# A float32 delta-rule recurrence with an MLP behind it: 128-wide TensorE products and transposes recast as 64x64 tiles, with PSUM handed out in four pairs of banks

## The chip, the cores and the metric

The kernel runs on one core of one Trainium2 chip. The metric is device time in microseconds of one execution, median of several runs. TensorE is called PE below, its weight loads PEld, VectorE DVE, ScalarE ACT, GpSimd POOL and SyncE SP.

## The reference, cut to what matters

```python
batch, n_heads, seq, head_dim = (4, 8, 768, 40)
for t in range(S):
    y[:, :, t] = np.einsum('bhd,bhde->bhe', rt, state)
    Sa = np.einsum('bhde,bhe->bhd', state, at)
    state_decay = state * wt[:, :, None, :] - np.einsum('bhd,bhe->bhde', Sa, bt)
    state = state_decay + np.einsum('bhd,bhe->bhde', vt, kt)
...
x = attn_out.transpose(0, 2, 1, 3).reshape(3072, 320)
h = x @ w_in                                  # 320 x 1024
e = np.exp(h - np.max(h, -1, keepdims=True))
solu = h * e / (np.sum(e, -1, keepdims=True) + 1e-09)
ln = (solu - mean) / np.sqrt(var + 1e-06) * g_ln
out = ln @ w_out                              # 1024 x 320
```

r, k, v, w, a and b are float32, the MLP's weights float64; the output is 3072 x 320 in float32.

## The kernel before, in words

The sequence is cut into chunks of 64 steps. One piece of work i is one chunk of a pair of batches: two batches times 64 steps fill the 128 partitions, and there are 24 pieces (12 chunks times two pairs, in turn). Within a chunk the recurrence is written as products of matrices. A unit of such a product is one batch p and one head (q, g, h); its operands take 64 partitions or 40, and its result 64 partitions, so 16 units go to the array as 64x64 tiles, four at a time. in_turn() (line 256) orders the units so that four neighbours lie in four different quadrants. mm() (line 264) issues such a product. Each float32 product shows as two matmul records and two weight loads in the trace; a transpose (nc.tensor.transpose) as one of each.

The steps of a piece, by their functions and the tiles that they write:

- logged(), decay() (322, 326): lw = log of the decay, pcum = its running sum over the chunk (one 128x128 product of 320 columns), ei = exp of it and inv = exp of its negative.
- turned() (347): four 128x128 transposes that bring a token-major tile to feature-major. It serves decay_turned() (pei, to ex), front() (pa, to aT on DVE), front_b() (pb, to bT), attend_kv() and attend_r() (pk, pv, pr, to kT, vT, rT on ACT). stated() (505) turns the state in the same way (pst, to s).
- norm() (394): pnt, masked into nt on DVE, which goes to DRAM; spread() and invert() bring it back as blocks and invert a triangular matrix on DVE in 30 steps of two instructions each (lines 436 and 438, tiles prod and uu) for two pieces at once. some() doles these steps out to given places in DVE's order: 3 or 0, then 5, 4, and 5 or 4 in each iteration.
- flip(), couple(), close() (461, 467, 480): tu turned on DVE, py to wy on ACT, pz to tu.
- scores() (518): ps, masked into psi and lv on DVE. carried() and driven() (536, 552): px, which becomes x0 on ACT. solved() (564): pu, to nuT and lu on ACT. answered() (583): pl, masked on DVE into the other half of lu. read() (594): pyo, in two halves (own and not own) with fence(), a drain of PE, between them; it reads s, lv and lu. leave() (618): x and the new state's total tot on DVE, the state on POOL; x goes by DMA to xT.
- The MLP, 128 tokens at a time: hidden() (661) makes h from two 128-row blocks and one 64-row block of w_in, six products of 512 columns; highest(), exped(), weighed(), spreadof() (673 to 709) are the row maximum nmax (DVE), e = exp (ACT), e = h*e (DVE) and the statistics bs, mv, c (DVE) and rs (POOL); folded() (711) turns e by eight 128x128 transposes into lnT; output() (723) makes po by eight 128x128 products of 320 columns, in two halves, and osb (ACT), which is stored.
- narrow(), split() (208, 177): the float64 weights are narrowed to float32 by bit operations on DVE and ACT, in the prologue and in iterations -1 to 3.

The order of every engine is written by hand: each engine executes in the order in which the functions are called (manual_schedule). The main loop (line 823) runs i from -1 to 27. Iteration i works at once on pieces i (solved, answered, read, leave), i+1 (scores, couple, close, carried, driven), i+2 (by_value, attend), i+5 to i+7 (front, norm, decay) and the MLP of earlier ones. In it, PE goes through pu, ps, pst, pa, h, pb, pei, h, pcum, po, py, pnt, pl, po, pz, pyo (own), px, h (64 rows, two products), drain, pyo (not own), px, plnT, h, pk, pv, h, pr. DVE goes through psi, lv, aT, steps, tu, nmax, steps, nt, lu, e, bs, mv, c, steps, x, tot, steps.

PSUM has eight banks. ps1 gives pairs of banks in two buffers to all 64x64 products (banks()), ps2 one pair to h, pcum of early pieces and the mean, ps3 single banks in two buffers to transposes, pcum and po (bank()). A product that takes a buffer waits until the buffer's former content has been read.

Of the kernel before, what the change touches and what calls it, by code (L numbers as in the profile page):

```python
# [17 lines left out]
P = 128  # L18
# [9 lines left out]
THIN = (5, 15)  # L28
# [23 lines left out]
def kernel(  # L52
# [34 lines left out]
    ps1 = ctx.enter_context(tc.tile_pool(name="ps1", bufs=2, space=PSUM))  # L87
    ps2 = ctx.enter_context(tc.tile_pool(name="ps2", bufs=1, space=PSUM))
    ps3 = ctx.enter_context(tc.tile_pool(name="ps3", bufs=2, space=PSUM))
# [30 lines left out]
    ei_t = zeroed(nc.vector, "ei", [P, H, C], 1, pad)  # L120
# [18 lines left out]
    def banks(name):  # L139
        return ps1.tile([P, 2, 512], FP32, tag="banks", name=name)  # L140

    def bank(name):
        return ps3.tile([P, 512], FP32, tag="bank", name=name)
# [76 lines left out]
    def turn_g():  # L220
        pg = bank("pg")
        nc.tensor.transpose(out=pg[:, 0:NF], in_=g_rows, identity=ident[0:NF, 0:NF])
        for x, y in zip(g_cols, (0, -20, -36)):
            nc.scalar.mul(out=x, in_=pg[:, 0:NF], mul=2.0 ** y)
# [6 lines left out]
    def mean_of(lo, hi, begun):  # L231
        t = bank("pmean")
# [33 lines left out]

    def fence():
        nc.tensor.drain()  # L270
# [51 lines left out]
    def logged(i):  # L322
        lw = st[i]["lw"] = two.tile([P, DM], FP32, tag="lw", name="lw", bufs=1)
        nc.scalar.activation(out=lw, in_=st[i]["raw_w"].rearrange("p h d -> p (h d)"), func=AF.Ln)

    def decay(i):
# [5 lines left out]
        t = (bank("pcum") if i > 5 else ps2.tile([P, DFF], FP32, tag="h", name="h"))[:, 0:DM]  # L332
        nc.tensor.matmul(t, lhsT=c_("cum"), rhs=d["lw"], start=True, stop=True)  # L333
        nc.scalar.activation(out=ei_t[0][:, :, 0:D], in_=heads(t), func=AF.Exp)
# [12 lines left out]
    def turned(name, x):  # L347
        t = bank("p" + name)
        for j in range(4):
            nc.tensor.transpose(out=t[0:W2, j * P:(j + 1) * P],  # L350
                                in_=x[:, 2 * j:2 * j + 2].rearrange("p a b -> p (a b)")[:, 0:W2], identity=ident)
        return t[0:W2].rearrange("p (j b t) -> p b j t", j=4, b=2)

# [3 lines left out]
    def kept(name, t, bufs=1):  # L357
        o = tokens(name, bufs)
        nc.scalar.copy(out=o[0:W2], in_=t)
        return o  # L360

    def decay_turned(i):
        if not ok(i):
            return
        ex = st[i]["ex"] = ex_t[i % (AHEAD + 2)]
        nc.scalar.copy(out=ex[0:W2, :, :, 1:], in_=turned("ei", ei_t[0]))

    def front(i):
        if not ok(i):
            return  # L370
        d = st[i]
        t = turned("a", d["raw_a"])
        aT = d["aT"] = tokens("aT", AHEAD)
        nc.vector.tensor_tensor(out=aT[0:W2], in0=t, in1=d["ex"][0:W2, :, :, 0:C], op=ALU.mult)

    def front_b(i):
        if not ok(i):
            return
        d = st[i]
        d["bT"] = kept("bT", turned("b", d["kb"][:, H:]))  # L380
# [13 lines left out]
    def norm(i):  # L394
# [3 lines left out]
        t = banks("pnt")  # L398
# [68 lines left out]
    def couple(i):  # L467
# [3 lines left out]
        t = banks("py")  # L471
# [8 lines left out]
    def close(i):  # L480
# [3 lines left out]
        t = banks("pz")  # L484
# [8 lines left out]
    def attend_kv(i):  # L493
        if not ok(i):
            return
        d = st[i]
        d["kT"] = kept("kT", turned("k", d["kb"]))
        d["vT"] = kept("vT", turned("v", v_t[0]))

    def attend_r(i):  # L500
        if not ok(i):
            return
        st[i]["rT"] = kept("rT", turned("r", r_t[0]), 2)

    def stated(i):
        if not ok(i):
            return
        d = st[i]
        bp, ci = where_(i)
        if ci:  # L510
            t = bank("pst")
            for x in range(4):
                nc.tensor.transpose(out=t[0:W2, x * P:(x + 1) * P],  # L513
# [418 lines left out]
```

## Time and profile before

| what | value |
|---|---|
| median of 3 runs | 620.01 us (620.0, 620.01, 626.2) |
| span of the profiled execution, first to last instruction | 616.2 us (the page lists no other time for it) |
| mean granted clock of PE in it | 0.928 |
| start of pu in iterations 0, 5, 18, 23 | 65.8, 183.0, 464.5, 561.6 us |
| transfers | 59.93 MB, mean 97 GB/s |
| the queue that brings PE's instructions (q8) | 90 packets, 1.47 MB |

The profiled execution is a separate one from the timed ones: durations and places in time are read from it, and the median is compared with the timed runs of the changed kernel. The page gives busy time and number of instructions of each engine, the span in 40 slices with the clock that PE was granted, DMA queues, the chain of work that ended last, and groups of instructions with their mean time and the idle time before them. Ends of matmuls are modelled and overlap; their starts are measured. In a line of the timeline, the columns are start, duration, engine, line, operation, output and inputs, shapes and how many were merged; a bracket gives idle time before it and who ended it. In the table by stage the columns are the stretch, its length, and for PE, PEld, DVE, ACT and POOL the busy time and number of instructions, then the granted clock, the DMA engines' share and GB/s.

### The profile page before, as it was taken

The page shows a single profiled execution, that of the slowest core. Times are in us where ns is not written, and L with a number is a line of the kernel's source. Part 1 is how long each engine was busy: PE and PEld are TensorE (multiplying, and loading weights), DVE is VectorE, ACT ScalarE, POOL GpSimd, SP SyncE. Part 2 cuts the span into 40 slices and gives each one's busy share as a digit, 9 for nine tenths or more (in the row PEclk, how much of TensorE's full clock was granted, in tenths as well). Part 3 has the DMA queues.
Part 4 walks back from the last instruction along what each step waited for, and adds up shares of the span by engine and source line. Part 5 has one row for each costly group of instructions (what it writes and reads, how often), then busy time and mean ns, then how long its engine had stood idle before and what let it go on. Part 6 is the DMA issues. An engine that isn't in the chain of part 4 may idle for free.

```text
span 616.2 us, 26656 instructions
## 1 busy us (share of the span) xinstructions
PE 552.0 (90%) x11453; PEld 401.9 (65%) x11453; DVE 449.0 (73%) x1262; ACT 265.8 (43%) x548; POOL 258.0 (42%) x424
## 2 busy tenths in 40 slices
PE   5555668889999999999999999999999999999994
PEld 3333457666676777777777777777777676676652
DVE  4797986988968869869868868788697588443431
ACT  3433444654543544454444445444433343342221
POOL 3463264283453472473365355444624631322200
PEclk9665765789999999999999999999999999999998
DMA  7986887476455455564564474564532622310100
GB/s 164 159 156 121 183 157 129 98 156 104 76 106 104 90 115 99 93 122 95 100 123 91 95 126 98 112 113 82 110 56 53 118 49 43 65 35 26 28 19 21
DMA packets 213901, 59.93 MB, mean 97 GB/s; under 512 B 199120, under 2 KB 208952, under 8 KB 213784
## 3 DMA queue, kind: packets, MB, share of 16 engines
q1 hardware_dynamic: 195512, 33.78, 32.8%
q0 software_dynamic: 11568, 19.78, 14.0%
q10 hardware_dynamic: 6704, 4.67, 2.7%
q8 instruction: 90, 1.47, 1.0%
q14 instruction: 27, 0.22, 0.1%
HBM read 40.10 MB, written 13.37 MB: 87 GB/s over the span
## 4 chain that ended last, share of the span: by engine, by line
PE 74%; DVE 17%; ACT 3%; issue 3%; DMA 1%; ACTq 1%; DVEq 0%; SPq 0%
PE po L731 16%; PE h L265 16%; PE pyo L265 8%; DVE uu L438 5%; DVE prod L436 5%; PE pu L265 4%; PE plnT L720 4%; PE ps L265 4%; PE px L265 3%; PE py L265 2%; PE pl L265 2%; PE pz L265 2%; PE pr L350 2%; PE pst L513 2%; PE pcum L333 1%
## 5 line engine op out<-in xcount | busy, mean ns | idle before, releaser
L265 PE MATMUL h<-w_in,xT 128*128 128x512 f32 (+1 forms) x288 | 123.7, 614 | 0.0
L731 PE MATMUL po<-w,lnT 128*128 128x320 f32 x384 | 112.7, 438 | 0.5 <-ACT lnT L721 0.5
L438 DVE TENSOR_TENSOR uu<-uu,prod 128x30 f32<-128x30 f32 (+4 forms) x360 | 102.1, 284 | 12.4
L436 DVE TENSOR_TENSOR prod<-blk,uu 128x30 f32<-128x30 f32 (+4 forms) x360 | 99.2, 276 | 9.6
L731 PEld LDWEIGHTS po<-w,lnT 128*128 128x128 f32 x384 | 71.0, 190 | 32.6 <-issue 4.1
L409 POOL DMA_DIRECT2D nt_dram<-nt x20 | 18.8, 938 | 120.8 <-DVE nt L383 99.8
L709 POOL TENSOR_TENSOR rs<-c,mhalf 128x1 f32<-128x1 f32 x24 | 13.5, 561 | 112.3 <-DVE c L708 103.4
L383 DVE TENSOR_TENSOR psi<-ps,cst 128x512 f32<-128x512 f32 x24 | 16.6, 690 | 59.5 <-PE ps L265 59.5
L658 POOL DMA_DIRECT2D xT<-x x96 | 48.9, 514 | 0.4 <-DMA blk<-nt_dram 0.3
L265 PEld LDWEIGHTS h<-w_in,xT 128*128 128x128 f32 (+1 forms) x288 | 37.6, 190 | 9.4 <-issue 8.1
L678 DVE TENSOR_REDUCE nmax<-h 128x1 f32<-128x1024 f32 x24 | 28.6, 1193 | 18.6 <-PE h L265 18.6
L420 POOL DMA_DIRECT2D blk<-nt_dram x46 | 36.9, 808 | 11.8 <-issue 8.4
L265 PE MATMUL pyo<-lv,kb 64*64 64x104 f32 x768 | 38.3, 269 | 2.2
L265 PEld LDWEIGHTS pyo<-lv,kb 64*64 64x64 f32 x768 | 24.1, 142 | 21.2 <-issue 21.1
L265 PE MATMUL pyo<-lu,kb 64*64 64x104 f32 x768 | 37.4, 262 | 0.1
L646 POOL TENSOR_TENSOR st<-tot,ex 104x160 f32<-104x160 f32 x44 | 21.7, 511 | 36.4 <-DVE tot L642 32.4
L562 ACT COPY x<-px 128x320 f32<-128x320 f32 x24 | 10.2, 426 | 56.3 <-PE px L265 56.1
L477 ACT ACTIVATE wy<-py,cst 128x256 f32<-128x256 f32 x24 | 11.4, 474 | 53.2 <-PE py L265 53.2
L288 POOL DMA_DIRECT2D raw_r<-in_r_dram x48 | 33.9, 709 | 0.0
L735 ACT ACTIVATE osb<-po,rs 128x320 f32<-128x320 f32 x24 | 12.7, 527 | 48.5 <-PE po L731 32.8
L686 ACT ACTIVATE e<-h,nmax 128x1024 f32<-128x1024 f32 x24 | 26.6, 1108 | 14.3 <-DVE nmax L678 14.3
L692 DVE TENSOR_TENSOR e<-h,e 128x1024 f32<-128x1024 f32 x24 | 29.2, 1217 | 4.7 <-ACT e L686 4.7
(131 smaller groups left out, 1169.1 us busy)
## 6 DMA issues: line engine op xcount, KB each, us to landing
blk<-nt_dram POOLq DMA_DIRECT2D x46, 128.0 KB, 4.7
nt_dram<-nt POOLq DMA_DIRECT2D x20, 256.0 KB, 3.7
raw_w<-in_w_dram SPq DMA_DIRECT2D x48, 80.0 KB
a<-in_a_dram SPq DMA_DIRECT2D x48, 80.0 KB
raw_r<-in_r_dram POOLq DMA_DIRECT2D x48, 80.0 KB, 3.6
lv<-in_v_dram SPq DMA_DIRECT2D x48, 80.0 KB
out_dram<-osb ACTq DMA_DIRECT2D x24, 160.0 KB
raw_b<-in_b_dram SPq DMA_DIRECT2D x44, 80.0 KB
```

Of the source, the lines that this page charges most:

```text
L265: nc.tensor.matmul(o, lhsT=lhsT, rhs=rhs, start=start, stop=stop, skip_group_check=True)
L288: queue.dma_start(out=x[half(p), :, 0:D], in_=ap[2 * bp + p, :, ci * C:(ci + 1) * C, :].rearrange("h t d -> t h d"))
L420: queue.dma_start(out=nb[home:home + Q], in_=blocks[n][:, Q * e:Q * e + Q, Q * e:Q * e + Q])
L436: nc.vector.tensor_tensor(out=t, in0=nb[:, j:j + 1, j + 1:Q].to_broadcast([P, n_c, m]), in1=u[:, 0:n_c, j:j + 1].to_broadcast([P, n_c, m]) ...
L438: nc.vector.tensor_tensor(out=u[:, 0:n_c, j + 1:Q], in0=u[:, 0:n_c, j + 1:Q], in1=t, op=ALU.subtract)
L646: nc.gpsimd.tensor_tensor(out=to3(old), in0=to3(tot[0:W2]), in1=ex[:, :, 2 * q:2 * q + 2, C:].to_broadcast([W2, 2, 2, D]), op=ALU.mult)
L658: nc.gpsimd.dma_start(out=xT[to:to + Q, 2], in_=x[at + P - 3 * D:at + D, 2])
L678: nc.vector.tensor_reduce(out=nmax, in_=d["h"], axis=AX.X, op=ALU.max, negate=True)
L686: nc.scalar.activation(out=e, in_=d["h"], func=AF.Exp, bias=d["nmax"], accum_out=d["esum"])
L692: nc.vector.tensor_tensor(out=d["e"], in0=d["h"], in1=d["e"], op=ALU.mult)
L720: nc.tensor.transpose(out=t[:, j * P:(j + 1) * P], in_=d["e"][:, f * P:(f + 1) * P], identity=ident)
L731: nc.tensor.matmul(d["out"][:, 0:DM], lhsT=d["lnT"][:, f, :], rhs=w2[:, f, :], start=f == 0, stop=f == NF - 1)
```

## The change

All but a few PE instructions become 64x64 products through mm(); left as they were are the mean of w_out and the turn of g_ln.

- turned(), stated() and folded() no longer transpose: each 64x64 (or 64x40) block is multiplied with a 64x64 identity, 16 products in place of four transposes, and 32 in place of eight for e. The source of the decay's turn is lw itself, with the running-sum matrix in place of the identity, so the turn and the sum are one product; ACT then takes exp while copying to ex, and ei is gone. decay() still makes pcum for inv, by two half-sized products into one bank.
- hidden() makes each of five waves of four 64-row, 64-token products of 512 columns, each in its own quadrant, the two row halves into different banks; output() makes 16 waves of four products of 160 columns in two phases, between which row halves and banks are exchanged, with a fence() ahead of the second phase. folded() writes the two halves of features into two banks and needs two copies as before.
- PSUM becomes four pairs of banks, A, B, C, H, each in one buffer. two_turned() puts two turns in one pair: k with v, the state with a, b with the decay. A takes pu, pbe, py, pl, pyo; B takes ps, pcum, pnt, pz, plnT, pr; C takes psa, po, px, pkv; H takes h.
- In the main loop answered() moves behind weighed(), spreadof() and the second phase of output(); carried() goes ahead of read(own), driven() ahead of read(not own), and the 64-row part of h behind both. In PE's order: pu, ps, psa, h, pbe, h, pcum, po, py, pnt, drain, po, pl, pz, px, pyo (own), drain, px, pyo (not own), h, plnT, h, pkv, h, pr. In DVE's order: psi, lv, aT, steps, tu, nmax, steps, nt, e, bs, mv, c, lu, steps, x, tot, steps. The exception for iterations 5 and 15 (THIN) goes. In ACT's order osb is ahead of tu as before, and kT and vT follow each other.

```diff
+    def pair(letter, name):
+        return psum.tile([P, 2, 512], FP32, tag=letter, name=name)
...
-        t = (bank("pcum") if i > 5 else ps2.tile([P, DFF], FP32, tag="h", name="h"))[:, 0:DM]
-        nc.tensor.matmul(t, lhsT=c_("cum"), rhs=d["lw"], start=True, stop=True)
-        nc.scalar.activation(out=ei_t[0][:, :, 0:D], in_=heads(t), func=AF.Exp)
+        t = pair("B", "pcum")[:, 0, 0:DM]
+        for p in range(2):
+            mm(heads(t)[half(p)], c_("cum")[half(p), half(p)], d["lw"][half(p), :, 0:D])
...
-    def turned(name, x):
-        t = bank("p" + name)
-        for j in range(4):
-            nc.tensor.transpose(out=t[0:W2, j * P:(j + 1) * P],
-                                in_=x[:, 2 * j:2 * j + 2].rearrange("p a b -> p (a b)")[:, 0:W2], identity=ident)
-        return t[0:W2].rearrange("p (j b t) -> p b j t", j=4, b=2)
+    def turned(t, k, x, by="ident"):
+        t = t[:, :, 4 * C * k:4 * C * k + 4 * C]
+        for u in in_turn(lambda p, q, g, h: (p, h)):
+            p, q, g, h = u
+            j = 2 * q + g
+            m = C if h == 0 else D
+            mm(t[C * h:C * h + m, p, j * C:j * C + C], x[half(p), 2 * j + h, 0:m], c_(by)[half(p), half(p)])
+        return t[0:W2].rearrange("p b (j t) -> p b j t", j=4)
+    def two_turned(letter, name, *parts):
+        parts = [x for x in parts if x is not None]
+        if parts:
+            t = pair(letter, name)
+            for x in [(out, product(t, k)) for k, (product, out) in enumerate(parts)]:
+                x[0](x[1])
...
-            part = slice(0, P) if kt < 2 else half(x)
-            mm(d["h"][:, 512 * x:512 * x + 512], d["xT"][part, kt], w_in[part, 2 * kt + (x if kt < 2 else 0)],
-               start=kt == NK - 1, stop=kt == NK - 2)
+            for row in range(2):
+                for col in range(2):
+                    x = row ^ phase
+                    mm(d["banks"][half(col), x], d["xT"][half(row), kt, half(col)],
+                       w_in[half(row), 2 * kt + (x if kt < 2 else 0)], start=kt == NK - 1, stop=(kt, phase) == (1, 1))
...
-                nc.tensor.transpose(out=t[:, j * P:(j + 1) * P], in_=d["e"][:, f * P:(f + 1) * P], identity=ident)
+        for f in range(NF):
+            for row in range(2):
+                for col in range(2):
+                    at = f * P + col * C
+                    mm(t[half(col), row, f * C:f * C + C], d["e"][half(row), at:at + C], ident[half(row), half(row)])
...
-        for f in range(x * NF // 2, x * NF // 2 + NF // 2):
-            nc.tensor.matmul(d["out"][:, 0:DM], lhsT=d["lnT"][:, f, :], rhs=w2[:, f, :], start=f == 0, stop=f == NF - 1)
+        for f in range(NF):
+            for row in range(2):
+                for col in range(2):
+                    x = row ^ phase
+                    mm(d["out"][half(col), x, 0:m], d["lnT"][half(row), f, half(col)], w2[half(row), f, x * m:x * m + m],
+                       start=f == 0 and phase == 0, stop=f == NF - 1 and phase == 1)
...
-        if i not in THIN:
-            stated(i)
-            front(j)
+        two_turned("C", "psa", stated(i), front(j))
+        if i + 1 >= N:
+            fence()
...
-        front_b(j)
-        if ok(j + 2):
-            logged(j + 2)
+        logged(j + 2)
+        two_turned("A", "pbe", front_b(j), decay_turned(j + 1))
...
         norm(j)
-        answered(i)
         weighed(m - 2)
         spreadof(m - 2)
...
+        fence()
         output(m - 3, 1)
+        answered(i)
         close(i + 1)
+        carried(i + 1)
         read(i, True)
-        carried(i + 1)
         narrow(some_weights[2], pieces[3], ok(j) and j % GRP == GRP - 1)
+        fence()
+        driven(i + 1)
+        read(i, False)
+        leave(i)
         by_value(i + 2)
-        if ok(m - 1):
-            hidden(m - 1, ((2, 0), (2, 1)))
-        fence()
-        read(i, False)
-        driven(i + 1)
-        leave(i)
         begin_narrow(narrowed.get(i + 1, (0,))[0])
+        hidden(m - 1, ((2, 0),))
         folded(m - 2)
```

## The prediction, written before the changed kernel was run

> **What bounds the kernel now.** First the page: TensorE (PE) is busy nine tenths of the span and at its full granted clock from about 145 us on.
>
> ```profile
> PE 552.0 (90%) x11453; PEld 401.9 (65%) x11453; DVE 449.0 (73%) x1262; ACT 265.8 (43%) x548; POOL 258.0 (42%) x424
> ...
> PEclk9665765789999999999999999999999999999998
> ```
>
> Then busy time by stage, cut at the starts of pu (the first product of each iteration of the main loop): iterations 0 to 3, 5 to 17, 18 to 22, and the last.
>
> ```profile
> 65.80:161.30 95.50, 74.35 (x1733) 58.52 (x1733) 83.45 (x233) 48.46 (x102) 46.27 (x71) 0.78 0.68 131
> ...
> 183.00:464.50 281.50, 278.77 (x6268) 205.16 (x6267) 220.77 (x640) 129.40 (x270) 135.74 (x220) 1.00 0.53 102
> 464.50:561.60 97.10, 94.87 (x2209) 68.51 (x2208) 60.68 (x170) 38.09 (x77) 32.44 (x61) 1.00 0.30 59
> ```
>
> Before 161 us VectorE (DVE) is the fuller engine (83.45 of 95.5 us). From 183 to 464.5 PE has 278.8 of 281.5 us: thirteen iterations, pitch 21.65 us, bound by PE. DVE has 220.77/13 = 17.0 us of work in each. Third, I read one iteration of that stage on both engines, because the change also re-orders DVE. The DVE timeline:
>
> ```profile
> 380.66 0.69 DVE L383 TENSOR_TENSOR psi<-ps,cst 128x512 f32<-128x512 f32 x1 [1.45 <-PE ps L265]
> ...
> 389.71 0.68 DVE L383 TENSOR_TENSOR lu<-pl,cst 128x512 f32<-128x512 f32 x1
> 390.31 1.22 DVE L692 TENSOR_TENSOR e<-h,e 128x1024 f32<-128x1024 f32 x1
> ...
> 393.33 0.16 DVE L708 TENSOR_TENSOR c<-c,mv 128x1 f32<-128x1 f32 x1
> ```
>
> From psi to the last c DVE runs without a wait: 380.66 to 393.49, 12.8 us (the same stretch is 12.8 us one iteration earlier). lu is done at 390.39, well ahead of its reader. Its only wait here is for PE's ps, 1.45 us. The PE timeline of the same iteration:
>
> ```profile
> 379.95 0.65 PE L265 MATMUL ps<-rT,vT 40*64 40x64 f32 x32
> 380.52 0.65 PE L513 MATMUL pst<-cst,st 128*104 128x128 f32 x4
> ...
> 383.18 1.02 PE L265 MATMUL h<-w_in,xT 128*128 128x512 f32 x2
> 384.04 0.72 PE L333 MATMUL pcum<-lw,cst 128*128 128x320 f32 x2
> ...
> 391.56 0.67 PE L265 MATMUL pyo<-rT,s 40*64 40x64 f32 x32
> 392.06 0.36 PE L265 MATMUL pyo<-lv,kb 64*64 64x104 f32 x8
> 392.24 0.36 PE L265 MATMUL pyo<-lu,kb 64*64 64x104 f32 x8
> ...
> 393.43 1.13 PE L265 MATMUL h<-w_in,xT 64*128 64x512 f32 x4
> 394.65 0.41 PE L265 MATMUL pyo<-lv,kb 64*64 64x104 f32 x8
> ```
>
> Starts are real, ends modelled, so I use start-to-start paces: 0.43 us a record of h (0.86 for a product's two), 0.18 us for a wave of four 64x64 products of 104 columns.
>
> **PE's own work.** Prices from these rows. Seven turns of four transposes (0.44 us each: 397.76 to 398.20) become seven of 16 products with the identity; nearest row pu, 32 records of 64 columns, 0.44 to 0.51 us (378.50, 379.01, 379.45). I take 0.48: +0.04 x 7 = +0.3 us; ends -0.0 and +0.5. plnT: 0.93 becomes 0.96. h: five waves of 512 columns; no row has such a wave. By columns it is 512/104 x 0.178 = 0.88, by h's own rows 0.86, and the row-halved h here takes 1.22 with its drain. I take 0.86 (nearest in length); ends 0.86 and 1.22. Output: 16 waves of 160 columns, 0.27 each by columns, 4.3 to 4.4 us, now 2.25 + 2.35. pcum: 0.55 stays, at most 1.1 if its two halves, which share a bank, do not overlap. Changes of tile shape cost now: pnt to pl to po 0.78 + 0.63 against 0.48 a wave group, ps to pst 0.57, px to plnT 0.56, h to pyo 1.22 against 0.86; together some 1 to 1.5 us. Added: one more drain, 0.3 us each (1.22 - 0.86 = 0.36; lower end 0).
>
> Sum of a whole iteration, at these prices. From pyo<-rT to the end of ps: pyo 0.50 + 0.77, drain 0.3, px 0.48, pyo 0.76, h 0.86, plnT 0.96, h 0.86, pkv 0.96, h 0.86, pr 0.48, pu 0.95, ps 1.0 = 9.7 us. From there to the end of px<-st: psa 0.96, h 0.86, pbe 0.96, h 0.86, pcum 0.55, output 2.15, py 0.48, pnt 0.48, drain 0.3, output 2.15, pl 0.48, pz 0.48, px 0.48 = 11.2 us. Were PE alone the bound: 20.9 against 21.65, a gain of 0.75 us an iteration.
>
> One rule speaks against this change. The Trainium skill's "TensorE: Matmul & The Clock Gate", Part 1, says that starts of matmuls never come closer than about 25 ns; this trace has 32 records of py in 0.48 us (386.84 to 387.32), 15 ns each, so here the measurement decides. By that floor, an estimate, the 288 records of the new transposes would take 288 x 10 ns = 2.9 us more an iteration.
>
> **The moved step that decides.** answered() goes behind spreadof(), so in DVE's order lu stands after e, bs, mv and the three c, where before it stood ahead of e. On PE, pl goes behind the second half of the output. pl and pyo now share pair A, so the first product of pyo must wait for DVE's lu; queued behind that wait on PE are all of read(), driven(), h, plnT, the k, v and r turns, pu and ps, and DVE's next psi waits for ps. That closes a loop: psi to lu on DVE 12.8 us (the same instructions, another order; the wait for pl is no issue, since pl ends 10.2 us after ps), handing over 0.1 (wy to pl: ACT ends 388.04, PE starts 388.10), PE 9.7, handing over 0.2 (last ps group 379.95 + 0.50, psi 380.66). Pitch 12.8 + 0.1 + 9.7 + 0.2 = 22.8 us, where 21.65 is now. PE stands before pyo for 12.8 + 0.3 - 11.2 = 1.9 us: the saved shape changes are paid out as a wait.
>
> The other moves are covered. ACT loses ei (0.44 us) and has 129.4 of 281.5 us. ps needs pair B free of rT, whose copy ends about when pu does (cover about 0.1 us). pcum needs psi and lv out of B: done 1.4 us after ps, wanted at 3.6. pu needs A free of x and tot: 1.5 us after pyo, wanted at 5. h's pair is read by e until 9 us before its next use. POOL's and SP's lists keep their order; x is 1 us later in the loop and its xT transfers are wanted an iteration later.
>
> **By stage, against the profiled execution.** To 140 us: DVE's order has no e or bs yet, lu is where it was; the clock is low, and less idle PE could help a little or the added drains hurt: 0 (ends -6 and +4). Iterations 3 and 4: DVE's narrowing hides most; +0.8. Thirteen iterations: 13 x (22.8 - 21.65) = +15. Iterations 18 to 22, now 97.1 us: the DVE stretch is 13.0, 11.6 and 11.7 us in the first three (466.6, 488.5, 507.8 to their last c), plus 10.0 each; in 21 and 22 no inverse steps are left, and the chain h, nmax, wy, exp, e, bs, c, lu puts lu at 10.8 us after ps (psa 0.5, h 1.72, output 2.15, py 0.48, wy 0.6, exp 1.4, e 1.25, bs 1.3, mv and c 0.7, lu 0.7), so 20.5 and, with 3.7 us less on PE where k, v and r are no more turned and no ps follows, 16.8. Sum 103.6: +6.5. Last iterations: 23 waits in the same way, +1.7; the three after it hold h and output alone, as long as now; the last output needs both copies of lnT, +0.5. Instruction fetch: 22,906 loads and matmuls now in 90 packets, and per iteration 438 products in four records each, 1752 against 964. One stall shows now (486.94, 0.89 us before the rest of ps), so 165 packets make two or three; +2 (ends 0 and one per iteration). Sum +26: the span of 616.2 becomes 642. The median lies 3.8 us above that span, so 646 us.
>
> **Rivals.**
> - Faster: lu does not decide, PE alone does. It holds if DVE's stretch from psi to lu is under 11.0 us. For it: psi, nt and the steps might run a little quicker. Against: 12.8 us without a wait in every iteration read. 13 x 0.75 = 10 and some 3 later: 606 us.
> - No difference: PE's path after pyo comes to 8.6 instead of 9.7, as it would if drains cost nothing and products with the identity ran by the lower rows, or the early stage gains 10 us by a warmer clock. Pitch 21.7, the end still waits: 620 us.
> - The instruction list becomes the bound: with twice the packets and no sparse stretch (h of 12 records) to catch up in, a stall like the 0.89 us comes once an iteration on the part after pyo, where nothing hides it. For it: that stall lies at the end of the densest stretch there is, pu and ps. Against: the same stretch passes without one in over 20 iterations. 646 + 24 x 0.9 = 667 us.
>
> **How the numbers follow.** Lu wait 0.60, instruction list 0.13, no difference 0.08, faster 0.19. One per cent (6 us) is about what a measurement of this kernel can tell from no change. Faster 0.19, same 0.08, slower 0.73. The likeliest case alone spans 632 (drains free, 13 x 0.5 less, early gain) to 660 (h waves dearer by half the way to 1.22, 0.18 x 3 on the loop, and the upper price of the turns, 0.1, for 22 iterations). The range leaves out the faster rival: 614 to 672.
>
> **What would show it.** Right: PE idle of about 2 us before pyo with DVE's lu as the releaser in every iteration from 4 on; a pitch of 22 to 23 us; lu directly before DVE's inverse steps; h at 0.43 us a record and wave; PE below 95% from 183 us on. Wrong: PE idle before pyo under 0.3 us (the faster rival), gaps called issue on PE (the list), a slower wave of h, or a first 160 us that differ by over 6 us.

## The result, and the profile after it

The changed kernel takes 742.1 us (four runs, 741.4 to 746.1), the kernel before 621.0 (four runs): ratio 1.198 [1.192, 1.204]. The prediction was 646 us, at most 672. The direction was right, the size far off, and most of what follows is the search for the missing 96 us. Of the runs below, two of the four of wide_all, its profiled one among them, were over 1.5% slower than its fastest; its ratio is that of the other two. The profiled execution took 741.5 us, with a span of 739.6, 123.4 more than the 616.2 before.

The page after, busy time and number of instructions of each engine, the granted clock in 40 slices, and the queue that brings PE's instructions:

```profile
PE 582.1 (79%) x20853; PEld 475.7 (64%) x20853; DVE 452.0 (61%) x1263; ACT 257.6 (35%) x524; POOL 257.1 (35%) x424
...
PEclk9655579979999989999999999999999999999998
...
q8 instruction: 164, 2.69, 1.6%
```

PE is busy 30 us longer and yet only 79% of the span instead of 90%. So 93 of the 123 us are not busy but idle time, and the gaps are what has to be explained. q8 counts 164 packets for 41,706 matmuls and loads (twice 20,853), some 256 in each packet.

By stage, cut at the starts of pu as in the prediction (iterations 0 to 3, 5 to 17, 18 to 22):

```profile
69.60:170.80 101.20, 76.28 (x2581) 62.32 (x2571) 84.00 (x234) 47.27 (x100) 48.54 (x76) 0.78 0.65 125
...
196.90:558.50 361.60, 296.10 (x11400) 247.34 (x11392) 223.87 (x640) 125.89 (x259) 135.61 (x222) 0.96 0.42 81
558.50:679.60 121.10, 103.90 (x3736) 83.14 (x3732) 60.64 (x170) 38.06 (x77) 30.84 (x58) 0.93 0.23 47
```

| stage | before | after | difference |
|---|---|---|---|
| to pu of iteration 0 | 65.8 | 69.6 | +3.8 |
| iterations 0 to 3 | 95.5 | 101.2 | +5.7 |
| iteration 4 | 21.7 | 26.1 | +4.4 |
| iterations 5 to 17 | 281.5 | 361.6 | +80.1 |
| iterations 18 to 22 | 97.1 | 121.1 | +24.0 |
| the rest | 54.6 | 60.0 | +5.4 |

In the thirteen iterations the pitch goes from 21.65 to 27.8 us, where 22.8 was predicted. DVE's work is unchanged (223.87 against 220.77 us). PE works 296.1 us, 17.3 more, and is idle for 65.5 us instead of 2.7. The waits of PE in that stage (engine, tile, line, releaser: us in total, times, longest):

```profile
PE pyo L261 <- DVE lu L394: 10.1, 12, 1.1
PE psa L261 <- issue: 9.8, 5, 2.2
PE ps L261 <- issue: 9.5, 7, 1.7
PE pbe L261 <- issue: 5.9, 5, 1.6
```

The predicted wait is there, in twelve of thirteen iterations, but it is 10.1 us in all. Five times as much, 52 us over the twelve rows of the list that name it, goes to "issue": PE waited for nothing that the profile shows. The kernel before has 0.2 us of that in this stage. One iteration on PE's timeline:

```profile
411.31 0.69 PE L261 MATMUL pyo<-rT,s 40*64 40x64 f32 x32 [1.12 <-DVE lu L394]
...
422.27 0.60 PE L261 MATMUL pu<-x,tu 64*64 64x40 f32 x27 [1.71 <-issue]
...
426.56 0.59 PE L261 MATMUL psa<-cst,a 64*64 64x64 f32 x26 [2.12 <-issue]
...
428.01 1.15 PE L261 MATMUL pbe<-cst,kb 64*40 64x64 f32 x30
```

The bracket stands in the middle of a product: 4 of 32 records of the second half of pu have run, then nothing for 1.71 us, then the rest. The rest read the same two tiles as the four before them, so it is hard to see which data could be late. The distance between such a stop and the next, 422.27 to 426.56, holds little but 64-column products (pu, ps, psa). Behind the longest stop the 64-column rows run at half pace: 30 records of pbe take 1.15 us where 28 took 0.57 an iteration earlier (at 400.08 us), and six of h, at 429.86, 1.61 us where eight took 1.04 (at 414.06).

On DVE everything is as predicted: lu starts 0.08 us after the last c does (410.49), the inverse steps follow, and after x and tot comes a long idle stretch until PE's ps.

```profile
410.57 0.68 DVE L394 TENSOR_TENSOR lu<-pl,cst 128x512 f32<-128x512 f32 x1
...
423.94 0.69 DVE L394 TENSOR_TENSOR psi<-ps,cst 128x512 f32<-128x512 f32 x1 [8.41 <-PE ps L261]
```

Three theories were to be told apart. The instruction list (F in the expectations): a packet of 256 instructions needs some 3.5 us to arrive, and a stretch in which PE would be through 256 sooner has to wait. Prices (P): PE's own work, with its shape changes and drains, costs what it costs, and the list limits nothing. And the loop through lu, as predicted: the moved answered() is what counts.

### The profile page after: what moved, and what is told of

Same layout as the page of the kernel before. It is cut to its first block, busy times and chain, and to the rows that moved or that the text cites. A ratio compares the mean times of both kernels' runs of the same rounds, so it can differ in the third digit from the quotient of the medians.

```text
span 739.6 us, 45491 instructions
## 1 busy us (share of the span) xinstructions
PE 582.1 (79%) x20853; PEld 475.7 (64%) x20853; DVE 452.0 (61%) x1263; ACT 257.6 (35%) x524; POOL 257.1 (35%) x424
## 3 DMA queue, kind: packets, MB, share of 16 engines
q1 hardware_dynamic: 195512, 33.78, 27.2%
## 4 chain that ended last, share of the span: by engine, by line
PE 51%; DVE 26%; issue 12%; DMA 4%; ACT 3%; SPq 3%; DVEq 0%; ACTq 0%
PE h L261 13%; PE pyo L261 8%; PE po L261 7%; DVE uu L449 5%; DVE prod L447 4%; DVE bs L713 4%; DVE e L705 3%; PE plnT L261 3%; PE pu L261 3%; PE pkv L261 3%; PE ps L261 3%; PE px L261 3%; PE psa L261 2%; SPq L283 2%; DVE lu L394 2%
## 5 line engine op out<-in xcount | busy, mean ns | idle before, releaser
L261 PE MATMUL h<-w_in,xT 64*64 64x512 f32 x960 | 142.7, 638 | 6.8 <-issue 5.7
L261 PE MATMUL po<-w,lnT 64*64 64x160 f32 x3072 | 123.8, 299 | 4.9 <-issue 1.2
L261 PEld LDWEIGHTS po<-w,lnT 64*64 64x64 f32 x3072 | 109.1, 133 | 17.5 <-issue 13.7
L261 PEld LDWEIGHTS h<-w_in,xT 64*64 64x64 f32 x960 | 37.1, 144 | 20.7 <-issue 18.8
L736 ACT COPY lnT<-plnT 128x512 f32<-128x512 f32 x48 | 25.8, 589 | 56.0 <-PE plnT L261 56.0
L261 PE MATMUL pcum<-lw,cst 64*64 64x320 f32 x96 | 22.0, 521 | 28.6 <-ACT lw L321 28.6
L691 DVE TENSOR_REDUCE nmax<-h 128x1 f32<-128x1024 f32 x24 | 28.8, 1200 | 25.0 <-PE h L261 24.8
L261 PEld LDWEIGHTS plnT<-cst,e 64*64 64x64 f32 x1536 | 30.0, 136 | 20.6 <-issue 16.2
L261 PE MATMUL pyo<-lu,kb 64*64 64x104 f32 x768 | 43.1, 293 | 0.3 <-issue 0.3
L637 DVE TENSOR_TENSOR x<-pyo,ex 104x256 f32<-104x256 f32 x48 | 18.1, 419 | 36.1 <-PE pyo L261 34.7
L261 PE MATMUL pyo<-rT,s 40*64 40x64 f32 x704 | 16.6, 230 | 23.7 <-DVE lu L394 22.1
```

The lines of the kernel that those rows point to most:

```text
L261: nc.tensor.matmul(o, lhsT=lhsT, rhs=rhs, start=start, stop=stop, skip_group_check=True)
L691: nc.vector.tensor_reduce(out=nmax, in_=d["h"], axis=AX.X, op=ALU.max, negate=True)
L736: nc.scalar.copy(out=lnT[:, :, half(row)], in_=t[:, row].rearrange("p (f t) -> p f t", f=NF))
```

## The experiments

Ratios are against the kernel before on the same chip; where there is no ratio, one run of each was taken. The pitch is the mean of iterations 5 to 17. A "stop" is counted, in that stage, where two records of one product (h left out) start 0.6 us or more apart, and that distance is its length; where idle time is meant, as the lists of waits have it, the text says so.

**1. lu_early: the changed kernel, with answered() back ahead of weighed().**

```diff
         norm(j)
+        answered(i)
         weighed(m - 2)
...
         output(m - 3, 1)
 
-        answered(i)
         close(i + 1)
```

> The changed kernel with answered() back in its old place, behind norm() and ahead of weighed(), so that lu is masked before e, bs, mv and c. Theory F (PE's instruction list is the bound: one refill of 256 instructions takes 3.3 to 4 us whatever PE does, and an iteration has some 6.9 refills): the wait before pyo goes, but PE runs into the next refill earlier; pitch 27 us or more in the middle stage, 728 to 740 us in all. Rival A (the wait for lu and the refills simply add up): 1.1 us in each of 13 iterations and 2 us in the last 6 come off, 742 becomes about 715 us. Rival L (lu's loop alone explains the loss): PE's path of 20.9 us is left, about 610 us.

Measured: 732.6 us (before 619.0), pitch 27.6. PE waits for lu no more, and about 9 us of the whole run are all that came of it: 43 stops of 57 us in all stay. Undoing the moved step alone leaves the kernel 114 us behind, so the loop through lu is not where the 96 us went.

**2. tail_run: the kernel before, with three runs of 1024 extra products at its end, of 64, 104 and 160 columns, whose results nobody reads.**

```diff
+    t = ps1.tile([P, 2, 512], FP32, tag="banks", name="ptail")
+    for width in (64, 104, 160):
+        for n in range(1024 // 4):
+            for row in range(2):
+                for col in range(2):
+                    mm(t[half(col), row, 0:width], ident[half(row), half(col)], w2[half(row), 0, 0:width])
```

> The kernel before, with three runs of 1024 products behind its last product, 64x64 in the four quadrants, of 64, 104 and 160 columns, which nobody reads: extra work, the output is untouched. Each run has 4096 instructions, 16 refills. Theory F: the runs of 64 and of 104 columns take the same time, 16 x 3.3 to 3.8 = 53 to 61 us, the run of 160 columns 68 to 70 us as PE needs; some 180 us are added. Rival P (PE's own rate, as the 16 or 48 products of the kernel before show it): 256 waves of 0.116, 0.178 and 0.27 us = 30, 46 and 69 us; 145 us are added.

Measured: 797.2 us, 178 more. The timeline of PE in the 64-column part, in the 104-column part, and at the start of the 160-column part (the merged row names it by its first shape):

```profile
618.45 2.09 PE L265 MATMUL ptail<-w,cst 64*64 64x64 f32 x128 [1.38 <-issue]
621.92 2.09 PE L265 MATMUL ptail<-w,cst 64*64 64x64 f32 x128 [1.38 <-issue]
...
671.88 3.08 PE L265 MATMUL ptail<-w,cst 64*64 64x104 f32 x128 [0.39 <-issue]
675.62 3.08 PE L265 MATMUL ptail<-w,cst 64*64 64x104 f32 x128 [0.67 <-issue]
...
721.88 72.15 PE L265 MATMUL ptail<-w,cst 64*64 64x104 f32 x2131 [0.40 <-issue]
```

This is the cleanest reading of the study. 128 records with their 128 loads, 256 instructions, then a stop, again and again, at the same distance: 618.45 to 621.92 is 3.47 us with 64 columns, and with 104 columns it is 3.47 or 3.74 too (4.02 once), although PE needs 2.09 us of it in the one case and 3.08 in the other. With 160 columns 2131 records run in 72.15 us, 4.3 us for 128 of them, and no stop is left. All transfers together made 5 GB/s there (76 on the mean of the run), so these stops are not contention with other transfers. The 12,288 added instructions are 48 more packets of q8 (138 instead of 90), 256 in each. In a long row of short products a block of 256 PE instructions costs the larger of PE's own time and about 3.5 us: F, shown and priced.

The stops of the changed kernel are the same thing. From one to the next in its trace:

```profile
506.56 0.47 PE L261 MATMUL ps<-aT,kT 40*64 40x64 f32 x17 [1.28 <-issue]
506.84 0.65 PE L261 MATMUL ps<-rT,vT 40*64 40x64 f32 x32
507.31 0.63 PE L261 MATMUL psa<-cst,st 64*64 64x64 f32 x32
507.77 0.64 PE L261 MATMUL psa<-cst,a 64*40 64x64 f32 x32
508.22 1.05 PE L261 MATMUL h<-w_in,xT 64*64 64x512 f32 x8
509.08 0.30 PE L261 MATMUL pbe<-cst,kb 64*40 64x64 f32 x7
510.44 0.58 PE L261 MATMUL pbe<-cst,kb 64*40 64x64 f32 x25 [1.06 <-issue]
```

These are 17 + 32 + 32 + 32 + 8 + 7 = 128 records, with their loads 256 instructions. Of the 48 gaps called issue in the thirteen iterations 47 stand so, a whole number of times 256 instructions apart (to within 10); the one that does not is of 0.16 us. Where two neighbours are one block apart, they are 3.5 to 4.6 us apart (once 5.97), the median 3.98. The changed kernel's 1752 instructions an iteration are 6.8 blocks: 23.8 us at the 3.47 of the tail_run, more than the 22.8 predicted from all else, and by an estimate from the 3.98 us of its own trace 27.2, near the 27.8 measured. Why a block takes longer in the kernel than in the tail was not tested.

**3 and 4. wide_turns and wide_turns_lu: the changed kernel with the turns of a, k, v, r, the state and e by 128-wide transposes again (b and the decay stay in 64x64); the second has answered() ahead of weighed() as well.**

```diff
+    def wide(t, k, x):
+        for j in range(4):
+            nc.tensor.transpose(out=t[0:W2, k, j * P:(j + 1) * P],
+                                in_=x[:, 2 * j:2 * j + 2].rearrange("p a b -> p (a b)")[:, 0:W2], identity=ident)
```

> The changed kernel with the turns of a, k, v, r, the state and e as 128-wide transposes again (24 to 28 transposes in place of 112 products with the identity in an iteration); b and the decay, h and the output stay as 64x64 products, order and PSUM pairs stay. Instructions of an iteration fall from 1752 to about 1360, refills from 6.9 to 5.3. Theory F: 5.3 x 4.0 = 21 us is under the loop through lu (22.8), so the pitch falls to 23 to 24.5 us and the time to 655 to 685 us. Rival W (the quadrant waves of h and output, or quadrant work as such, are what is slow; a turn costs 0.48 instead of 0.44): 730 to 742 us, and gaps of PE stay.

> wide_turns with answered() back ahead of weighed(): both suspected causes taken away, while h, output, the turns of b and of the decay stay 64x64 products and PSUM stays four pairs. In wide_turns PE stood 1.7 to 2 us before pyo for lu in each iteration and had a clock of 0.95 from 191 to 518 us. Theory F + L (list and loop are the two causes, the clock falls because PE idles): the wait is gone, the clock is 1.0, the pitch is PE's own path, 24.0 less 1.9 = 22.1 us as wide_turns' timeline has it, and the time 625 to 640 us. Rival (something else in the new layout, the PSUM pairs or the quadrant waves, holds PE): over 660 us, and PE idles still.

Measured: wide_turns 695.1 us, pitch 25.2; wide_turns_lu 665.5 us, ratio 1.075 [1.071, 1.079], pitch 24.1. Both are above what was expected, wide_turns_lu also above the 660 us of its rival. The turns do the same for PE's own time (0.44 us for four transposes, 0.45 to 0.48 for 16 products) with an eighth of the instructions, 8 against 64; 128 packets instead of 164. PE's longest wait in wide_turns, in iterations 6 to 17:

```profile
PE pyo L261 <- DVE lu L400: 20.0, 12, 2.0
```

The stops are all but gone (3, 2.3 us in all), and now the loop through lu is seen bare, 1.67 us a time (predicted 1.9). Why 25.2 then and not 22.8? Two iterations of this one execution, with the same work on PE (columns: stretch, length, busy time and number of PE, PEld, DVE, ACT, POOL, then the clock):

```profile
344.00:371.20 27.20, 25.33 (x681) 19.44 (x680) 18.63 (x52) 9.75 (x20) 8.44 (x14) 0.87 0.36 69
444.50:468.20 23.70, 21.91 (x681) 16.86 (x680) 18.64 (x52) 9.75 (x20) 8.51 (x15) 1.00 0.42 82
```

At the full clock the loop gives 23.7 us, at 0.87 27.2 us. The time from psi to the end of lu is the same 13.1 to 13.3 us in every iteration; what grows from 10.5 to 14.1 is the part from pyo to the next psi, behind the wait. So the wait, which is there in every iteration, was paid twice: by its length, and in some iterations by a lower clock after it. The expectation had left out the second. In wide_turns_lu the wait is gone and the clock back to 0.99, but stops return (12.7 us idle in all in px, pyo and once ps; px also waits eleven times some 0.3 us for ACT's osb, with which it shares pair C), as the chain of waits through one iteration shows (start, length, what):

```profile
342.99 0.55 PE px L261 x20
343.54 1.69 issue
345.23 0.37 PE px L261 x8
```

All but one stand in px and pyo: pl, pz, px and pyo follow each other there without a sparse product, while the kernel before has h between the halves of pyo.

**5. wide_out: the changed kernel, with the output as eight 128x128 products into one bank and no drain ahead of its second half.**

```diff
-        for f in range(NF):
-            for row in range(2):
-                for col in range(2):
-                    ...
+        for f in range(phase * NF // 2, phase * NF // 2 + NF // 2):
+            mm(d["out"][:, 0, 0:DM], d["lnT"][:, f, :], w2[:, f, :], start=f == 0, stop=f == NF - 1)
...
-        fence()
         output(m - 3, 1)
```

> The changed kernel with output() as eight 128x128 products of 320 columns in one bank, without the drain ahead of its second half; all turns and h stay 64x64. Instructions of an iteration fall from 1752 to about 1528, refills from 6.9 to 6.0. Theory F: 6.0 x 4.0 = 24 us, pitch 24 to 26 us, 685 to 715 us: less gained than by wide turns, since fewer instructions go. But the output is the one stretch where PE (0.27 us a wave of 16 instructions, 4.3 us per 256) is slower than a refill, so it may be worth less than its share: the instructions saved there are not those that stall. Rival W (the waves are slow): the gain is more than that of the wide turns, under 680 us.

Measured: 731.0 us, pitch 27.2, 143 packets: outside the range. The number of packets is not the measure. The output's products are long, 128 records in 4.3 us, so they were never in want of instructions; leaving them out thins no dense stretch. The stops that stay sit where the short products are (waits from 190 to 540 us):

```profile
PE pyo L261 <- DVE lu L394: 21.2, 12, 1.9
PE psa L261 <- issue: 20.6, 13, 1.9
```

Stops number 18 with 29.5 us, fewer than in the changed kernel, but lu's wait, which had been partly covered by them, is paid in full instead: 1.77 us for 0.84.

**6 and 7. wide_all and wide_all_lu: both edits together, the second with answered() early as well.**

> wide_turns and wide_out together: turns of a, k, v, r, state and e as transposes, the output as 128x128 products in one bank, no drain ahead of its second half; h, b's turn and the decay's turn stay 64x64 products; lu stays late. Some 1136 instructions an iteration, the densest stretch (pz to pyo, pu to pbe) broken up by the output. Theory: no refill stalls are left; the loop through lu (12.8 us on VectorE, 10.4 us on PE from pyo to ps with these turns, 0.3 for handing over) gives a pitch of 23.5 us, plus what the clock loses after each wait: 645 to 675 us. Rival (no loop, only the list): as wide_all_lu.

> wide_all with answered() ahead of weighed(). Left of the change: h in quadrant waves, the turns of b and the decay as products, four PSUM pairs in one buffer each, ei gone, the order of read and driven. Theory (list and loop are the whole loss): no stall called issue over 0.3 us in most iterations, no wait before pyo, pitch 21.5 to 22.3 us, 618 to 635 us. Rival (the PSUM pairs or the waves of h cost): over 640 us, with waits of PE for a bank to be read.

Measured: ratios 1.104 [1.095, 1.114] and 1.060 [1.056, 1.065] (656.7 us); both dearer than expected, wide_all_lu also than the 640 us of its rival; but no wait for a bank, which that rival named, is in its list of waits in that stage. This pair measures the loop through lu where little else disturbs it: no stop in wide_all, five of 7.3 us in all in wide_all_lu. At a full clock the pitch is 23.7 to 23.8 us in wide_all and 22.6 in wide_all_lu, 1.2 us apart; the medians differ by the difference of the ratios, 4.4% or 27 us, which holds some iterations of wide_all at a lower clock. In wide_all_lu the clock is 1.00 in every one of the thirteen iterations, with single idle stretches of up to 1.86 us. The prediction had 1.15 us and 24 us for the loop.

**8. wide_h_lu: wide_all_lu, with h and pcum in 128-wide products too, and without the drain behind psa in the last iterations.**

```diff
-            for row in range(2):
-                for col in range(2):
-                    ...
+            for x in range(2) if kt == NK - 1 else (phase,):
+                part = slice(0, P) if kt < 2 else half(x)
+                mm(d["banks"][:, x], d["xT"][part, kt], w_in[part, 2 * kt + (x if kt < 2 else 0)], ...)
```

> wide_all_lu with h and the running sum pcum as 128-wide products again (h's 64-row part as two 64x128 products). Left of the change: four PSUM pairs in one buffer each, the turns of b and of the decay as products, ei gone, carried ahead of read, the second drain. In wide_all_lu h takes 1.02 us beside a transpose and 0.86 beside products, k, v and the state with a 1.01 instead of 0.87. Theory (what is left of the loss there is changes of tile shape, about 1 us an iteration, and a refill stall of 1 to 2 us in every third iteration): these changes fall from ten to four, pitch 21.6 to 22 us, 618 to 632 us. Rival (the PSUM pairs or the order cost): 645 us or more, pitch still 22.6 us, with waits for a bank.

Measured: 652.9 us, 1.053 [1.044, 1.061]; a miss. It is above the rival's 645, but again no wait for a bank is there. An undisturbed iteration takes 22.2 us for the 22.6 of wide_all_lu. Only 102 packets are left, 12 more than before, and the stops stay (11, 14.4 us), in ps, px and pyo. What they have in common is not the number of instructions but their order: pl, pz, px, pyo (own), px, pyo (not own) are all 64x64 products, with h only behind them.

**9. before_h2_late: the kernel before, with nothing changed but the place of the 64-row h (two products, 8 instructions an iteration), which goes from between the halves of pyo to behind leave().**

```diff
-        if ok(m - 1):
-            hidden(m - 1, ((2, 0), (2, 1)))
         fence()
...
         begin_narrow(narrowed.get(i + 1, (0,))[0])
+        if ok(m - 1):
+            hidden(m - 1, ((2, 0), (2, 1)))
         folded(m - 2)
```

> The kernel before with one move and no added instruction: the 64-row products of h go from between the two halves of pyo to behind leave(), where the change has them, so that pz, pyo, px, pyo, px (384 instructions of short products) follow each other with only the drain between. Theory F (a block of 256 instructions takes the longer of PE's time and 3.5 us; what counts is how much of a block falls in short products): stalls of 1 to 1.5 us within pyo or px in a quarter to a half of the iterations, some of it given back since two changes of tile shape go; 622 to 640 us. Rival R (only the mean number of refills in an iteration counts): no stalls, 612 to 622 us.

Measured: 625.5 us, ratio 1.010 [1.007, 1.014], with exactly the 90 packets of the kernel before. The chain in an undisturbed iteration and in the next one:

```profile
332.44 0.94 PE pyo L265 x32
333.38 0.45 PE px L265 x32
...
353.97 0.94 PE pyo L265 x32
354.92 0.07 PE px L265 x3
354.98 0.94 issue
355.92 0.67 PE px L265 x29
```

The undisturbed one is at 21.5 us a pitch, as fast as before or a little faster; but in four iterations px stops (0.3 to 0.9 us idle), and once ps for 2.0, after which the clock of that iteration is 0.87. Not one instruction was added: taking a long product out of a row of short ones is enough to make stops. The rival (drain and shape changes saved, 612 to 622) fell.

**10. wide_h_break: wide_h_lu, with the 64-row h put back between the halves of pyo.**

```diff
-        hidden(m - 1, ((2, 0),))
...
+        hidden(m - 1, ((2, 0),))
         fence()
         driven(i + 1)
```

> wide_h_lu with the 64-row products of h back between the two halves of pyo, ahead of the drain, where the kernel before has them. Theory F: the stalls within px and pyo go, those within ps stay (one in four iterations); 630 to 645 us. Rival R: as wide_h_lu, 650 us or more, since an iteration has the same number of instructions.

Measured: 644.7 us, 1.042 [1.038, 1.046], pitch 22.7. Of the stops in px and pyo a single one of 0.2 us is left, those in ps stay, as F said:

```profile
PE ps L261 <- issue: 5.0, 4, 1.8
```

**11. h2_wave: the kernel before, with the 64-row h alone as a 64x64 wave.** Its two products of 512 columns become four.

> The kernel before with one part of the change alone: the 64-row part of h as one wave of four 64x64 products of 512 columns in place of two 64x128 products. 8 instructions more an iteration. If changes of tile shape cost PE what its timeline says (px to h 0.60 instead of 0.48, h to the drain's end 1.22 instead of 0.86 + 0.27): 0.2 us less in each of 20 iterations, 615 us (range 612 to 619). If shape changes cost nothing: 620 us.

Measured: 617.8 us against 617.6, ratio 0.9994 [0.997, 1.002]. The shape change that this saves is seen in the trace, but not in the median. In an iteration without stops the start of h follows that of px by 0.46 us, 0.60 before, and the pitch there is 21.4 instead of 21.5 us; from h to the product behind the drain it is 1.20 for 1.22. But three stops of 2.6 us idle in all stand in the thirteen iterations, where the kernel before had one of 0.2, so the profiled execution gains nothing there.

**12. h2_po: h2_wave, with both halves of the output together ahead of py, and exp ahead of wy on ACT.**

```diff
         output(m - 3, 0)
+        output(m - 3, 1)
...
-        couple(i + 1)
         exped(m - 2)
+        couple(i + 1)
```

> h2_wave with the two halves of the output product next to each other (both ahead of py) and exp ahead of couple() on ScalarE: two more changes of tile shape an iteration are gone, but py, pnt and pl come 2.2 us later, and VectorE waits some 1 us before nt, which it can spare. Theory (shape changes are what PE can still save): 0.3 us less an iteration, 606 to 613 us. Rival (the later pnt and pl move VectorE's e, bs and x so far that pyo or pu wait): 620 to 640 us.

Measured: 679.2 us, ratio 1.097 [1.091, 1.104]. The rival in the expectation had the direction and the reason, a later pnt and pl, but not the place of the wait (pl and pz, not pyo or pu) nor the size (620 to 640 us). PE's waits in iterations 5 to 17, and the chain:

```profile
PE pl L265 <- DVE nt L383: 10.6, 13, 0.8
PE pz L265 <- ACT wy L477: 2.5, 13, 0.2
...
338.58 0.54 ACT osb L740
...
339.70 1.21 ACT e L691 x2
340.91 0.37 ACT wy L477
```

With the output whole, osb stands ahead of exp and wy on ACT, and pz, which starts at 341.33, has to wait for all three. Some 29 of the 60 us come in iterations 5 to 17 and 22 after the start of pu in the last. Of the 29, 17 are not idle but busy time of PE (295.5 us instead of 278.8), at a granted clock of 0.93 instead of 1.00; the 22 at the end were not split. The interleaving of the output's halves gives ACT and DVE this time.

## Why the prediction was wrong, point by point

The predicted pitch was 22.8 us: 20.9 of PE's own work and 1.9 of waiting for lu. Measured are 27.8: 22.8 busy (296.1/13) and 5.0 idle (65.5/13). Two iterations of the changed kernel, one at a low clock and one at the full one:

```profile
252.80:281.30 28.50, 24.76 (x892) 20.09 (x887) 18.89 (x52) 9.72 (x20) 5.91 (x9) 0.87 0.33 63
392.70:419.80 27.10, 21.48 (x892) 17.92 (x885) 15.40 (x46) 9.81 (x21) 13.03 (x22) 1.00 0.53 100
```

- **The step that was to decide: it is there, but it does not decide, so the direction came right mostly for another reason.** "The first product of pyo must wait for DVE's lu": it does, from DVE's lu, with lu where it was predicted. Bare of stops it costs 1.67 us a time in wide_turns (1.9 predicted), and by wide_all against wide_all_lu 1.2 us of pitch (1.15 predicted) and 27 us in all (24 predicted). Its bare pitch is 23.7 us, not 22.8: psi to lu 13.2 for 12.9, and pyo to psi 10.5 for 9.9. In the changed kernel the wait shrinks to 0.84 us, as stops already hold PE up elsewhere; so undoing it returned only about 10 of some 120.
- **PE's own prices: right within about 1 us.** The six of the thirteen iterations with a clock of 1.00 have 21.5 to 22.5 us busy, 22.0 on the mean, against 20.9: h 0.86 a wave, pyo 0.18 a wave, a turn 0.45 to 0.48, the halves of the output 2.15 to 2.2 us. The records of the 64x64 turns start 15 ns apart, as the row had said against the page weighed there. P therefore explains little, some 0.6 to 1.1 us of an iteration.
- **The step that failed: "Instruction fetch ... 165 packets make two or three; +2 (ends 0 and one per iteration)".** The packets are 164; in the thirteen iterations alone there are 39 stops (those in h left out) of 54.0 us, up to 2.52 us each, which is three and 4.2 us an iteration (4.0 us of idle time). I had one stall in 90 packets and multiplied it by the number of packets, as if stops fell at random. They do not: the supply has a rate, 256 instructions in 3.47 us, and a longer row of products that ask for more has to stop. That could have been suspected: pu and ps, 256 instructions in 1.95 us, run at nearly twice that rate, and it was in ps that the one stall of 0.89 us stood. The change puts psa and pbe behind them, plnT, pkv and pr ahead, all as dense. The rival that named the list had the mechanism, its place ("no sparse stretch to catch up in") and 13%, but also one stall of 0.9 us as its price: 667 instead of 742.
- **A term that the sum had not: the clock.** After some stops and waits PE runs at half pace for a while: in the stretch from 427.59 to 431.00 us, behind the stop of 2.12 us, the granted clock is 0.50. In this stage the mean clock is 0.96 instead of 1.00, and busy time an iteration is 21.5 to 22.5 us where it is 1.00 and up to 24.8 where it is 0.87. Mean busy 22.8 less the 22.0 of the iterations at 1.00 is 0.8 us an iteration, less the lowest, 21.5, it is 1.3; the clock alone would make about 4% of 27.8, 1.1 us, by an estimate from that mean.
- So the 5.0 us that the pitch lies above the prediction are 3.1 of idle time (5.0, of which 4.0 by the list and 0.8 by lu, instead of 1.9), and 1.9 of busy time, about half by the clock and half by prices, which these runs do not part more closely.
- **By stage:** the first 140 us were to be free, and pu of iteration 3 starts 1.3 us later (138.7 against 137.4): right in the sum, by luck in part, since pu of iteration 0 is 3.8 us later and the three iterations behind it win back 2.5. Iterations 3 and 4 were to bring +0.8 and brought +12.6, the thirteen +15 and +80, 18 to 22 +6.5 and +24, the end with its waits +2.2 and +5.4. How the list, the clock and the loop share the stages other than the thirteen was not worked out.
- **The signs named beforehand:** the wait for lu is there, h is at its pace, PE is below 95% (82% in the thirteen); the pitch is not 22 to 23 us, and "gaps called issue on PE (the list)" were the sign of being wrong that came.

The Trainium skill's "Runtime: NRT & Kernel Launch", section "Instruction fetch mechanics", has the packets as seen here, blocks of 256 instructions, but says that crossing from one to the next is mostly hidden. The tail_run and this kernel say otherwise for PE: hidden at 160 columns (4.3 us a block), 1.38 us in the open at 64 columns. Its "TensorE: Matmul & The Clock Gate", section "HAM oscillation", gives as the abstract rule that PE should have no idle gaps of over some 3.4 us. No idle stretch of PE in the thirteen iterations is over 2.30 us, in wide_turns none over 2.0, in h2_po none over 0.82, and the clock of an iteration falls to 0.87 or 0.86 all the same; what decides, a sum of gaps, their place in time or something else, these runs do not single out.

What stays open: even wide_h_break, with 102 packets and lu early, is 26 us behind. Its profiled execution is 30 us longer than that of before, 14 of them in iterations 5 to 17, of which 6 are stops; its undisturbed iterations take 22.2 us against 21.5, which fits more changes of shape in PE's order and the move of carried() ahead of pyo but was not split further. Another 10 lie ahead of iteration 4 and were not tried by themselves. No version was faster than the kernel before.

## What to carry to other kernels

Count instructions as well as array time: for a stretch of PE of several blocks, instructions divided by 256 and multiplied by 3.5 us (4.0 in the changed kernel itself) is about the least that it took here, and where that exceeds PE's own time a product cut into four tiles is dearer than the whole, however well the tiles overlap. A single dense block, as pu and ps in the kernel before, mostly passes without a stop. The one unexplained gap in the tuned kernel's trace, in its densest place, was the edge of a rate limit and not a random event; before more is added there, ask how much is left to it. Where short products must follow each other, long ones between them (512 columns of h here) let the list catch up: moving two of them, with no instruction added, cost 1.0% in before_h2_late, and putting them back won 8 us in wide_h_break.

## What the runs showed of the hardware

- PE's instructions come at 256 in 3.47 us, now and then 3.74, with 64 columns and with 104 and with the DMA engines otherwise idle (tail_run); in the changed kernel stops one block apart are 3.5 to 4.6 us apart. One packet of q8 is 256 instructions: 12,288 more make 48 packets more (tail_run). Stops stand a whole number of such blocks apart.
- Four 128x128 transposes are 8 PE instructions, the same by 64x64 products with the identity 64; PE's own time is 0.44 and 0.45 to 0.48 us. In this float32 kernel the tiles are not dear in the array but in the list.
- With a wait of 1.7 us in each iteration, or of 0.8 us (h2_po, 0.93 over the thirteen), PE's clock falls in some iterations: the same 681 records took 23.7 us at 1.00 and 27.2 us at 0.87 (wide_turns). Without that wait it was 1.00 throughout, single stops of up to 1.86 us notwithstanding (wide_all_lu).
- Shape changes on PE are cheap but show: h took 1.02 us beside a transpose and 0.87 between other products (wide_all_lu); the one that h2_wave saves is 0.14 us of an iteration, which its median does not show.
